# Loading x tile 2 through GpSimd's queue, and v of tile 0 ahead of tile 2's transposes, in a fused attention and gated feed-forward kernel

## The chip, the cores and the metric

The kernel runs on one core of one Trainium2 chip. The metric is the device time of one execution in microseconds. In the text PE is the matrix engine, ACT is ScalarE, DVE is VectorE, POOL is GpSimd and SP is SyncE, as the profile names them.

## The reference

The reference takes x of shape 1 x 2048 x 512 in bf16 and normalises it over its last axis. It then adds three things: x itself, a linear attention with 32 heads, and a gated feed-forward block.

```python
def _A_ref(x, wqkv, w_phi, wo):          # H = 32 heads of 16
    q, k, v = ...                        # x @ wqkv, split into heads
    pq, pk = q @ w_phi, k @ w_phi        # per head
    phi_q = concat(softmax(pq), softmax(-pq)); phi_k = the same of pk
    kv = einsum("bhsf,bhsd->bhfd", phi_k, v)
    num = phi_q @ kv; den = phi_q . sum_s(phi_k) + 1e-6
    return (num / den) @ wo

def _B_ref(x, w_gate, w_up, w_down):     # F = 1792
    return ((x @ w_gate) * (x @ w_up)) @ w_down

xn = _layernorm(A_x)
return A_x + _A_ref(xn, A_wqkv, A_w_phi, A_wo) + _B_ref(xn, B_w_gate, B_w_up, B_w_down)
```

## The kernel before

The 2048 tokens are cut into 16 tiles of 128 tokens, and the tiles are loaded into one buffer `xall`. Everything that PE multiplies needs the normalised tokens transposed (`xnT`), with the 512 features on the partitions in four blocks of 128. Four tiles form a group of 512 tokens for the feed-forward part.

The work is written in the order in which each engine runs it: inside the manual schedule the engines execute their instructions in program order, and semaphores make them wait for one another. SP is one of these engines and issues nearly all loads.

The start handles tiles 0 to 3 in a special way, because nothing else can run until they are there:

- `dma_x` (L69) loads x tiles. SP's queue issues tile 0, then tile 2, then the two halves of `wv` (L75), then the first columns of `wg` and `wu` (L72), `wphi` and the other weights. ACT's queue issues tiles 1 and 3.
- POOL builds the identity matrix `ident` for the transposes and the block pattern `BO`. PE runs warm-up matmuls on constants (`warm_up`, L308).
- The sum of each tile goes to `tots`. DVE makes the sums of tiles 0 and 3 (L373). ACT makes those of tiles 1 and 2 as a by-product of a pass whose output is thrown away (`junk`, L377).
- `sub_sum` (L337, DVE) writes 512 x minus the sum into `xn`. The scale of 512 and the standard deviation are divided out later.
- `lt(n, lo, hi, copy)` transposes blocks lo to hi of tile n on PE into a PSUM bank `tp` (L205) and copies them to `xnT` (L206) on the engine that `copy` names, ACT if none is named.
- `first_v(n, js)` runs matmuls of tile n with the blocks js of `wv` (L236). The results of tiles 0 and 1 lie in the banks that later hold the kv sums, so they carry the name `kv` in the profile; those of tiles 2 and 3 are called `pv`.
- `stats_of` (L153, L342), `scales_of` (L345, L347) and `more_scales_of` (L350, L351) make the true scale `rs` on DVE and POOL, and `first_v_out` (L361, L363) copies v with that scale.
- `make_bd` (L212, POOL) and `fold` (L225, L232) fold `w_phi` into the key weights `W1k`.

After that the feed-forward units `ffn` (one unit is four `g` matmuls, L274, four `u` matmuls, L278, a copy and a product) alternate with the projections of keys, values and queries, and then with attention and the output `fin` (L290, L293).

PSUM banks come from a ring of six (`bank`), and each new name takes the next one. The part of the start whose order matters here is:

```python
sum_of(0)
for n in (1, 2):
    nc.scalar.activation(out=junk[:], in_=xall[:, n, :], func=AF.Identity, accum_out=tots[n][:])
...
sub_sum(1, tots[1])
lt(0, 0, 2)
lt(0, 2, DC, nc.vector.tensor_copy)
lt(1)
warm_up(1)
sub_sum(2, tots[2])
sum_of(3)
sub_sum(3, tots[3])
lt(2)
for n in range(3):
    first_v(n, (0, 1))
lt(3)
```

Of the kernel before, what the change touches and what calls it, by code (L numbers as in the profile page):

```python
# [8 lines left out]
BF16 = mybir.dt.bfloat16  # L9
F32 = mybir.dt.float32  # L10
AF = mybir.ActivationFunctionType
# [10 lines left out]
def kernel(  # L22
# [12 lines left out]
    nc = tc.nc  # L35
    P = 128
    S, D = A_x.shape[-2], A_x.shape[-1]
# [4 lines left out]
    DC = D // P  # L42
# [10 lines left out]
    consts = ctx.enter_context(tc.tile_pool(name="consts", bufs=1))  # L53
# [4 lines left out]
    wv = wpool.tile([P, DC, D], BF16)  # L58
# [9 lines left out]
    def dma_x(lo, hi, eng=nc.sync):  # L68
        eng.dma_start(out=xall[:, lo:hi, :], in_=x_view[:, lo:hi, :])  # L69
# [1 line left out]
    def dma_cols(eng, w, src, lo, hi, at=0):  # L71
        eng.dma_start(out=w[:, :, lo - at:hi - at], in_=src[:, lo:hi].rearrange("(c p) f -> p c f", p=P))  # L72

    def dma_wv(lo, hi):
        nc.sync.dma_start(out=wv[:, lo:hi, :],  # L75
                          in_=A_wqkv[lo * P:hi * P, 2 * D:3 * D].rearrange("(c p) f -> p c f", p=P))

    def dma_gu(lo, hi):
        dma_cols(nc.sync, wg, B_w_gate, lo, hi)
        dma_cols(nc.sync, wu, B_w_up, lo, hi)  # L80

    dma_x(0, 1)
    dma_x(2, 3)
    dma_wv(0, 2)
    dma_wv(2, DC)
    dma_gu(0, 2 * P)
    nc.sync.dma_start(out=wphi[:], in_=A_w_phi.rearrange("(c h) d f -> (h d) c f", c=DC))
    dma_gu(2 * P, 5 * P)
# [5 lines left out]
    nc.sync.dma_start(out=wd[:], in_=B_w_down.rearrange("(c p) d -> p c d", p=P))  # L94
    nc.sync.dma_start(out=wo[:], in_=A_wo.rearrange("(c p) n -> p c n", p=P))

    ET = mybir.EngineType
    ctx.enter_context(tc.manual_schedule(engines={ET.PE, ET.DVE, ET.Activation, ET.Pool, ET.SP}))
    ones = nc.const_aps.tensor(1.0, [P, P], BF16)
    first = consts.tile([P, 1], BF16)  # L100
    nc.scalar.activation(out=first[:], in_=ones[:, 0:1], func=AF.Exp, scale=1.0)
    dma_x(1, 2, nc.scalar)
    dma_x(3, 4, nc.scalar)
    ident = consts.tile([P, P], BF16)
    make_identity(nc, ident[:])
    mhalf = consts.tile([P, GT], F32)
# [38 lines left out]
    def bank(name, dt=F32, n=TT):  # L145
        return ps_s.tile([P, n], dt, name=name, tag="s")
# [55 lines left out]
    def lt(n, lo=0, hi=DC, copy=nc.scalar.copy):  # L202
        tp = bank("tp", BF16).rearrange("p (c t) -> p c t", c=DC)
        for c in range(lo, hi):
            nc.tensor.transpose(out=tp[:, c, :], in_=xns[n][:, c * P:(c + 1) * P], identity=ident[:])  # L205
        copy(out=xnT[:, lo:hi, n * P:(n + 1) * P], in_=tp[:, lo:hi, :])  # L206
# [27 lines left out]
    def proj(ps, n, w, js=range(DC)):  # L234
        for j in js:
            nc.tensor.matmul(ps, lhsT=xnT[:, j, n * P:(n + 1) * P], rhs=w[:, j, :],  # L236
                             start=(j == 0), stop=(j == DC - 1))
# [68 lines left out]
    def warm_up(k, reps=DC):  # L306
        for _ in range(k):
            nc.tensor.matmul(warm[:, 0:reps * P], lhsT=ones,  # L308
                             rhs=nc.const_aps.tensor(1.0, [P, reps * P], BF16), start=True, stop=True)

    warm_up(7)
    warm_up(3, 1)

    with tc.tile_pool(name="ps_k", bufs=1, space=PSUM) as ps_k:
        kvbank = [ps_k.tile([P, TT], F32, name=f"kv{b}") for b in range(2)]
# [20 lines left out]
        def sub_sum(n, tot, lo=0, hi=D):  # L336
            nc.vector.tensor_scalar(out=xns[n][:, lo:hi], in0=xall[:, n, lo:hi], scalar1=float(D), scalar2=tot[:],  # L337
                                    op0=ALU.mult, op1=ALU.subtract)
# [14 lines left out]
        def first_v(n, js):  # L353
            if n not in vps:
                vps[n] = kvbank[n][:] if n < 2 else bank("pv")
            proj(vps[n], n, wv, js)
# [15 lines left out]
        def sum_of(n):  # L372
            nc.vector.tensor_reduce(out=tots[n][:], in_=xall[:, n, :], axis=AX.X, op=ALU.add)  # L373
# [4 lines left out]
        sub_sum(0, tots[0], 0, D // 2)  # L378
        sub_sum(0, tots[0], D // 2, D)
        sub_sum(1, tots[1])  # L380
        lt(0, 0, 2)
        lt(0, 2, DC, nc.vector.tensor_copy)
        lt(1)
        warm_up(1)
        sub_sum(2, tots[2])
        sum_of(3)
        sub_sum(3, tots[3])
        lt(2)
        for n in range(3):
            first_v(n, (0, 1))  # L390
        lt(3)
        first_v(0, (2, 3))
# [130 lines left out]
```

## Time and profile before

| what | value |
|---|---|
| median of 3 runs | 220.69 us (220.66 to 221.0) |
| the profiled execution | 220.62 us |
| its span | 218.9 us |
| PE busy | 214.9 us, 98% of the span |
| DVE busy | 140.6 us, 64% |
| ACT busy | 89.8 us, 41% |
| POOL busy | 74.1 us, 34% |
| granted TensorE clock | 1.0 |
| HBM read and written | 8.67 MB and 2.10 MB |

The span runs from the first to the last instruction of the program that the profiler recorded; the rest of the execution's time, 1.7 us, lies around it. Busy shares are averages over the span, so an engine with a small share can still be waited for at one place. A line number such as L205 is a line of the kernel before, and it can be the line of a helper that several callers use.

### The profile page before, as it was taken

The page shows a single profiled execution, that of the slowest core. Times are in us where ns is not written, and L with a number is a line of the kernel's source. Part 1 is how long each engine was busy: PE and PEld are TensorE (multiplying, and loading weights), DVE is VectorE, ACT ScalarE, POOL GpSimd, SP SyncE. Part 2 cuts the span into 40 slices and gives each one's busy share as a digit, 9 for nine tenths or more (in the row PEclk, how much of TensorE's full clock was granted, in tenths as well). Part 3 has the DMA queues.
Part 4 walks back from the last instruction along what each step waited for, and adds up shares of the span by engine and source line. Part 5 has one row for each costly group of instructions (what it writes and reads, how often), then busy time and mean ns, then how long its engine had stood idle before and what let it go on. Part 6 is the DMA issues. An engine that isn't in the chain of part 4 may idle for free.

```text
span 218.9 us, 3494 instructions
## 1 busy us (share of the span) xinstructions
PE 214.9 (98%) x1293; PEld 103.1 (47%) x1293; DVE 140.6 (64%) x239; ACT 89.8 (41%) x160; POOL 74.1 (34%) x71
## 2 busy tenths in 40 slices
PE   7999999999999999999999999999999999999994
PEld 3444445454444444444544444444444444454443
DVE  4868867886598758576599773296655655454321
ACT  6645686569575875565435212141231322100000
POOL 2540843363358554636045333033123033000000
PEclk9999999999999999999999999999999999999999
DMA  6999996003202540202028455114441431612301
GB/s 200 273 301 374 372 235 111 15 0 51 48 0 49 51 91 5 48 3 48 1 41 103 77 114 114 39 24 96 96 75 24 95 72 27 97 48 72 75 24 48
DMA packets 48529, 19.91 MB, mean 91 GB/s; under 512 B 37504, under 2 KB 48512, under 8 KB 48512
## 3 DMA queue, kind: packets, MB, share of 16 engines
q1 hardware_dynamic: 48224, 19.42, 39.7%
q10 hardware_dynamic: 288, 0.26, 0.3%
q8 instruction: 10, 0.16, 0.3%
q14 instruction: 7, 0.06, 0.1%
HBM read 8.67 MB, written 2.10 MB: 49 GB/s over the span
## 4 chain that ended last, share of the span: by engine, by line
PE 96%; DMA 1%; ACT 1%; DVE 0%; issue 0%
PE g L274 22%; PE fin L290 22%; PE u L278 22%; PE fin L293 6%; PE k L236 6%; PE q L236 6%; PE pv L236 6%; PE kv L330 2%; PE ab L462 2%; DMA xall<-in_A_x_dram 1%; PE kv L236 1%; ACT junk L377 1%; PE pq L225 1%; PE tp L205 0%; DVE xn L337 0%; DVE o_sb L300 0%
## 5 line engine op out<-in xcount | busy, mean ns | idle before, releaser
L274 PE MATMUL g<-xnT,wg 128*128 128x512 bf16 x224 | 57.5, 379 | 0.0
L278 PE MATMUL u<-xnT,wu 128*128 128x512 bf16 x224 | 57.5, 379 | 0.0
L282 DVE TENSOR_TENSOR hT<-u,g_sb 128x512 bf16<-128x512 f32 x56 | 37.0, 667 | 24.3 <-PE u L278 16.2
L253 POOL TENSOR_TENSOR phiq<-e,rsum 128x1024 bf16<-128x1024 f32 x16 | 30.9, 1933 | 63.5 <-DVE rsum L251 56.0
L281 ACT CAST g_sb<-g 128x512 bf16<-128x512 f32 x56 | 32.9, 587 | 47.1 <-PE g L274 46.9
L249 DVE TENSOR_REDUCE sums<-e 128x64 f32<-128x1024 f32 x32 | 38.9, 1216 | 20.1 <-ACT e L246 20.1
L290 PE MATMUL fin<-wd,hT 128*128 128x512 bf16 (+2 forms) x238 | 51.1, 366 | 0.0
L253 POOL TENSOR_TENSOR phik<-e,rsum 128x1024 bf16<-128x1024 f32 x16 | 30.9, 1932 | 40.0 <-DVE rsum L251 37.9
L278 PEld LDWEIGHTS <-wu 128*128 128x128 bf16 x224 | 21.9, 98 | 26.4
L290 PEld LDWEIGHTS <-hT 128*128 128x128 bf16 x238 | 22.5, 98 | 24.7
L274 PEld LDWEIGHTS <-wg 128*128 128x128 bf16 x224 | 21.1, 98 | 24.0
L236 PEld LDWEIGHTS <-xnT 128*128 128x128 bf16 x192 | 17.5, 98 | 18.3 <-ACT xnT L206 0.3
L300 DVE TENSOR_TENSOR o_sb<-fin,xall 128x512 bf16<-128x512 f32 (+2 forms) x13 | 8.5, 651 | 20.5 <-PE fin L293 20.5
L251 DVE RECIPROCAL rsum<-sums 128x64 f32<-128x64 f32 x32 | 17.7, 553 | 3.1
L293 PE MATMUL fin<-wo,oT 128*128 128x512 bf16 (+2 forms) x68 | 16.6, 366 | 0.0
L236 PE MATMUL k<-W1k,xnT 128*128 128x512 bf16 x64 | 16.4, 379 | 0.0
L236 PE MATMUL q<-W1q,xnT 128*128 128x512 bf16 x64 | 16.4, 378 | 0.0
L245 ACT ACTIVATE e<-q 128x512 f32<-128x512 f32 x12 | 7.2, 597 | 22.2 <-PE q L236 22.2
L236 PE MATMUL pv<-wv,xnT 128*128 128x512 bf16 x56 | 14.4, 379 | 0.0
L475 DVE TENSOR_TENSOR otok<-ab,rden 128x512 bf16<-128x512 f32 x16 | 11.1, 692 | 0.6
L322 ACT CAST vt<-pv 128x512 bf16<-128x512 f32 x12 | 7.0, 587 | 10.0 <-PE pv L236 10.0
L153 DVE BATCH_NORM_STATS2 stats<-xall 128x6 f32<-128x512 bf16 x16 | 10.6, 665 | 0.0
(62 smaller groups left out, 130.6 us busy)
## 6 DMA issues: line engine op xcount, KB each, us to landing
out_dram<-o_sb SPq DMA_DIRECT2D x15, 128.0 KB, 2.0
wd<-in_B_w_down_dram SPq DMA_DIRECT2D x1, 1792.0 KB, 15.5
xall<-in_A_x_dram SPq DMA_DIRECT2D x1, 1024.0 KB, 11.4
wg<-in_B_w_gate_dram SPq DMA_DIRECT2D x1, 640.0 KB, 8.5
wu<-in_B_w_up_dram SPq DMA_DIRECT2D x1, 640.0 KB, 9.7
wv<-in_A_wqkv_dram SPq DMA_DIRECT2D x2, 256.0 KB, 4.1
xall<-in_A_x_dram SPq DMA_DIRECT2D x1, 512.0 KB, 4.3
wg<-in_B_w_gate_dram SPq DMA_DIRECT2D x1, 512.0 KB, 5.2
```

Of the source, the lines that this page charges most:

```text
L153: nc.vector.bn_stats(out=stats[:], in_=xall[:, n, :])
L236: nc.tensor.matmul(ps, lhsT=xnT[:, j, n * P:(n + 1) * P], rhs=w[:, j, :], start=(j == 0), stop=(j == DC - 1))
L249: nc.vector.tensor_reduce(out=sums[:], in_=ev, axis=AX.X, op=ALU.add)
L251: nc.vector.reciprocal(out=rsum[:].rearrange("p a b -> p (a b)"), in_=sums[:])
L253: nc.gpsimd.tensor_tensor(out=phi[:].rearrange("p g (x f) -> p (g x) f", f=DH), in0=ev, in1=rsum[:].to_broadcast((P, 2 * H, DH)), op=ALU.mult)
L274: nc.tensor.matmul(gps, lhsT=wg[:, c, f * P:(f + 1) * P], rhs=xnT[:, c, T * TT:(T + 1) * TT], start=(c == 0), stop=(c == DC - 1))
L278: nc.tensor.matmul(ups, lhsT=wu[:, c, f * P:(f + 1) * P], rhs=xnT[:, c, T * TT:(T + 1) * TT], start=(c == 0), stop=(c == DC - 1))
L281: nc.scalar.copy(out=g_sb[:], in_=gps)
L282: nc.vector.tensor_tensor(out=hTs[T][:, f, :], in0=ups, in1=g_sb[:], op=ALU.mult)
L290: nc.tensor.matmul(ps, lhsT=hTs[T][:, f, t4 * P:(t4 + 1) * P], rhs=wd[:, f, lo:lo + w], start=(f == 0), stop=False)
L293: nc.tensor.matmul(ps, lhsT=oTs[n][:, c, :], rhs=wo[:, c, lo:lo + w], start=False, stop=(c == DC - 1))
L475: nc.vector.tensor_tensor(out=o_tok[:].rearrange("p (b h d) -> p b h d", b=2, d=DH), in0=abv[:, :, :, 0:DH], in1=rden[:].to_broadcast((P, ...
```

## The change

Tile 2 of x is no longer issued by SP but by GpSimd's queue, as that engine's first instruction of the kernel's own. SP's queue therefore issues the two halves of `wv` right behind tile 0, and the manual schedule begins ahead of the other loads. The two halves of tile 0's transposes swap the engines that copy them. The first two matmuls of v of tile 0 go ahead of the transposes of tile 2. These are done in two halves, the first copied by ACT and the second by DVE, and DVE's copy lies between its sum and its subtraction of tile 3. Two more short warm-up matmuls are run at the start.

```diff
-    def dma_wv(lo, hi):
-        nc.sync.dma_start(out=wv[:, lo:hi, :],
-                          in_=A_wqkv[lo * P:hi * P, 2 * D:3 * D].rearrange("(c p) f -> p c f", p=P))
+    def dma_wv(lo, hi, eng):
+        eng.dma_start(out=wv[:, lo:hi, :],
+                      in_=A_wqkv[lo * P:hi * P, 2 * D:3 * D].rearrange("(c p) f -> p c f", p=P))
...
     dma_x(0, 1)
-    dma_x(2, 3)
-    dma_wv(0, 2)
-    dma_wv(2, DC)
+    dma_wv(0, 2, nc.sync)
+    dma_wv(2, DC, nc.sync)
+
+    ET = mybir.EngineType
+    ctx.enter_context(tc.manual_schedule(engines={ET.PE, ET.DVE, ET.Activation, ET.Pool, ET.SP}))
+    ones = nc.const_aps.tensor(1.0, [P, P], BF16)
+    first = consts.tile([P, 1], BF16)
+    nc.scalar.activation(out=first[:], in_=ones[:, 0:1], func=AF.Exp, scale=1.0)
+    dma_x(1, 2, nc.scalar)
+    dma_x(3, 4, nc.scalar)
+    dma_x(2, 3, nc.gpsimd)
     dma_gu(0, 2 * P)
...
     warm_up(7)
-    warm_up(3, 1)
+    warm_up(5, 1)
...
-        lt(0, 0, 2)
-        lt(0, 2, DC, nc.vector.tensor_copy)
+        lt(0, 0, 2, nc.vector.tensor_copy)
+        lt(0, 2, DC)
         lt(1)
         warm_up(1)
+        first_v(0, (0, 1))
         sub_sum(2, tots[2])
+        lt(2, 0, 2)
         sum_of(3)
+        lt(2, 2, DC, nc.vector.tensor_copy)
         sub_sum(3, tots[3])
-        lt(2)
-        for n in range(3):
+        for n in (1, 2):
             first_v(n, (0, 1))
         lt(3)
         first_v(0, (2, 3))
```

More of the change, by code (lines that the diff above doesn't have):

```diff
@@ L95 @@
     nc.sync.dma_start(out=wo[:], in_=A_wo.rearrange("(c p) n -> p c n", p=P))
[L97 to L103, printed above, removed]
     ident = consts.tile([P, P], BF16)
```

## The prediction

> **What bounds the kernel now.** I read the page first, then the chain of waits in order of time up to 9.6 us, then the timelines of PE, ACT and DVE from 3 to 7 us, then the DMA answers for the first loads.
>
> The page's slices and its chain by engine:
>
> ```profile
> PE   7999999999999999999999999999999999999994
> ...
> PE 96%; DMA 1%; ACT 1%; DVE 0%; issue 0%
> ```
>
> PE is full in every slice but the first and the last, and the chain that ended last is 96% PE. So only the piece ahead of the first feed-forward matmul can still move. The chain through that piece (start, length, what):
>
> ```profile
> 0.85 2.74 DMA xall<-in_A_x_dram
> ...
> 3.61 0.46 ACT junk L377
> 4.07 0.08 issue
> 4.15 0.19 ACT junk L377
> 4.34 0.02 issue
> 4.37 0.73 ACT junk L377 x2
> 5.10 0.05 issue
> 5.15 0.36 DVE xn L337
> 5.51 0.05 issue
> 5.55 0.40 PE tp L205 x4
> 5.95 0.86 PE kv L236 x4
> ```
>
> x tile 1 lands at 0.85 + 2.74 = 3.59; ScalarE sums tile 1, then tile 2 (`junk`); VectorE subtracts the mean of tile 2; PE transposes tile 2 at 5.55, and from there PE never waits. Tile 2 itself was there earlier: issued on SP at 1.24, 2.8 us to landing, so 4.04, while ScalarE got to it at 4.37. PE's timeline around the last hole:
>
> ```profile
> 5.12 0.38 PE L308 MATMUL warm<-const-bfloat16-1.0 128*128 128x512 bf16 x1
> 5.55 0.40 PE L205 MATMUL tp<-ident,xn 128*128 128x128 bf16 x4
> ...
> 9.46 1.03 PE L274 MATMUL g<-xnT,wg 128*128 128x512 bf16 x4
> ```
>
> Matmuls of 512 columns follow each other every 0.216 us (four in 0.86), transposes every 0.056. After the warm-up matmul PE is free at 5.12 + 0.216 = 5.33 and idles 0.22 until 5.55. From 5.55 to 9.46 it runs 16 matmuls and 8 transposes: 3.45 + 0.45 = 3.90. From 9.46 on PE runs 206 us without a wait for data, so the change is worth what it moves the start of the first `g` from 9.46, one for one, unless it opens a hole behind.
>
> **The change, part by part.** *v of tile 0 ahead of tile 2's transposes.* Two matmuls (0.43) go into the hole: 5.33 to 5.76. Tile 2's `xn`, ready at 5.55, then waits for PE instead of the other way round, and 14 matmuls and 8 transposes remain: 3.02 + 0.45 = 3.47. The first `g` starts at 5.76 + 3.47 = 9.23, a gain of 0.22 to 0.23. That needs three things at 5.3: the last warm-up, columns 0 and 1 of `xnT` for tile 0, and the first half of `wv`.
>
> *Copies of tile 0 swapped.* The half that v of tile 0 needs first goes to DVE. Before, DVE copied at 4.94 (0.29) and ACT at 5.00 (0.35), ACT being held by its sum of tile 2. Now DVE can copy right behind the subtraction of tile 1, which starts at 4.48 and takes 0.35: about 4.8 to 5.1, ahead of 5.3. DVE's next step, the subtraction of tile 2, waits for ScalarE until 5.15 anyway. Cost nothing; if that copy came behind the ACT sum as before, it would be ready at 5.35, and 0.05 would be lost.
>
> *wv earlier on SP.* Its first half is issued at 1.24 instead of 1.71 (3.9 us to landing, so 5.61 before). The DMA engines decide, not the issue:
>
> ```profile
> 1.80:2.20 0.40, 0.40 (x3) 0.14 (x1) 0.00 (x0) 0.39 (x2) 0.33 (x2) 1.00 0.38 128
> 2.20:2.60 0.40, 0.40 (x3) 0.12 (x2) 0.00 (x0) 0.09 (x1) 0.20 (x1) 1.00 0.79 274
> 2.60:3.00 0.40, 0.40 (x3) 0.13 (x2) 0.00 (x0) 0.00 (x0) 0.00 (x0) 1.00 1.12 333
> ```
>
> The last two columns are DMA share and GB/s: unfilled until 2.6, full after. Before, four x tiles and the first half of `wv` (768 KB) had landed by 5.61, `wv` last. Now `wv` follows x0 at once and shares with x1, x3 and x2 instead of following x2. It cannot be later than 5.61 if the engines stay as full, and if three queues share evenly its data is through some 0.4 to 0.6 us before that: I take a landing at 5.1, bounds 4.8 and 5.6. Up to 5.3 it costs nothing; at 5.6 v of tile 0 starts at 5.65 instead of 5.33, and the sum is +0.1 instead of -0.22.
>
> *x2 through GpSimd's queue.* No row shows a load issued there. GpSimd's first own work starts at 0.78, so the issue is near that. Lower bound: 2.5 us to landing, x0's row, gives 3.3. Upper bound: the longest small load of the start, `wphi` (16 KB, 4.8), gives 5.6. I take 3.5, the longest x row (3.1) plus 0.4 for 128 KB at 333 GB/s among three sharers, because the x rows have the same bytes at the same moment: 4.3. ScalarE reaches tile 2 at 4.37; from landing to tile 2's transposes the rows give 5.55 - 4.37 = 1.18. So no cost up to a landing of 5.76 - 1.18 = 4.57 (from 4.37 to there PE is busy with v of tile 0), none compared with before up to 9.46 - 3.47 - 1.18 = 4.80, and one for one from there: 0.82 slower at the bound of 5.6. Behind the issue on GpSimd are `ident` (done at 1.35, first used at 4.42: 3 us of room) and `BO` (done at 2.40, needed by `bd` at 12.27).
>
> The rows show VectorE idle from 1.62, the end of its five memsets, to 3.36. The Trainium skill, page "SBUF — State Buffer", section "SBUF: two separate sides", says that a DMA from GpSimd's queue waits while VectorE is in a two-port mode, since GpSimd cannot write the descriptors then. No run here shows it yet; it stands as a rival below.
>
> *x1 and x0 among three queues.* By 2.6 the SP queue had moved 114 packets and ScalarE's 53; 80 packets then left in 0.2 us. x1 has some 75 left: at a half share 0.44 us, at a third 0.56, so x1 lands about 0.1 later (bounds 0 and 0.2). The subtraction of tile 1 and the transposes and warm-up behind it slip by 0.05, and tile 2's `xn` is ready at 5.65, still hidden by v of tile 0. ScalarE's copy of tile 1 ends near 6.0, where v of tile 1 wants it: 0.02 more. Together I charge 0.07.
>
> *Tile 2's copy on two engines.* The ACT half costs 0.35 instead of 0.58; v of tile 2 wants it at 6.45 and gets it at 6.4 to 6.5. The DVE half (0.29) stands between the sum and the subtraction of tile 3, so `xn` of tile 3 comes at 6.8 instead of 6.48; PE wants it at 6.9. Hidden; without that cover 0.29 at most. The statistics behind it on DVE shift by 0.3, and with them GpSimd's scales, the v copies on DVE (last end 11.77) and `bd` (end 13.35, needed at 14.74). DVE waits 0.82 for PE before its product at 13.19, which swallows the shift.
>
> *The rest.* Two more warm-ups of 128 columns cost 0.11 in a hole from 4.14 to 4.42: nothing. SP's later issues wait, as far as I read the gap from 4.84 to 5.62 that ends as `wv` lands, for an earlier load's signal; the second weights may so be issued up to 0.8 later, against use at 12.9 and landings near 10 to 11: nothing.
>
> Sum: -0.22 + 0.07 = -0.15. The profiled execution took 220.62 (span 218.9 and 1.7 around it), 0.07 under the median of 220.69; so 220.47 by it, 220.54 by the median. I say 220.5.
>
> **The rivals.**
>
> *Tile 2 arrives late (slower).* The place is ScalarE's sum of tile 2, the point 4.80, the price one for one, up to +0.82. For it: the whole chain from 4.37 to 5.55 hangs on this tile, the path is unmeasured, and now every ScalarE copy of tiles 0 and 1 queues behind that sum. If GpSimd's descriptors had to wait for the last VectorE memset at 1.62, x2 would land 0.84 later, at 5.14: +0.34. (That is the rule of the page "SBUF — State Buffer" of the Trainium skill.) With a slower queue on top, 5.3 to 5.6: +0.5 to +0.8, 221.2 to 221.5. Against it: VectorE is idle when the transfer should run. Chance 0.24, two thirds of it beyond 5.24, where the loss passes 0.2%.
>
> *v of tile 0 waits for wv.* Put ahead of the transposes, it now blocks them. With the engines full, `wv` could still be last, at 5.6: +0.1, 220.8. Against it: it is issued 0.46 earlier and shares evenly. Chance 0.09.
>
> *More than the hole.* If the unfilled DMA time before 2.6 is used by the third queue and x0 and x1 both land 0.25 earlier, the whole front moves: -0.47, 220.2. Against it: x0's packets start at 1.8 whatever stands in the other queues. Chance 0.07.
>
> **How the numbers follow.** The forecast, a gain between 0 and 0.25, has 0.60. 0.2% is 0.44 us, about what a measurement of this kernel can tell from no change. Faster by more: 0.07, the last rival. Slower by more: 0.16, from late tile 2. Within: 0.60 + 0.09 + 0.08 = 0.77. The range goes from 220.3 (best gain, and the spread of the runs) to 221.1 (tile 2 at 5.24); the likeliest case alone would be 220.4 to 220.7.
>
> **What would show it.** Right: PE's transposes of tile 2 start behind two `kv` matmuls near 5.8 and the first `g` near 9.3; PE without a hole after 5.4; x2 landing before 4.6 and `wv` before 5.3. Wrong: `junk` of tile 2 starting after 4.6 with DMA as its releaser (tile 2 late); an idle PE ahead of `kv` ended by DMA (`wv` late); the hole between transposes of tile 0 and of tile 1 growing (x0, x1 late); a hole ahead of `tp` of tile 3 ended by DVE (the copy split). The forecast also falls if PE shows a hole after 9.5, or if the time around the span changes from 1.7.

## The result and the profile after

The changed kernel takes 221.44 us (median of 17 runs, 221.09 to 222.28) against 221.0 for the kernel before (17 runs, 220.41 to 221.21). The ratio over all these runs is 1.0026, 95% interval 1.0017 to 1.0035, which is 0.57 us of 221; the medians lie 0.44 apart. The three runs that the prediction started from (220.69) lay low in the spread of the kernel before.

The profiled execution took 221.36, span 219.7. From here a line of the kernel before has a number higher by one or so (L377 is now L378). The chain of waits of the changed kernel up to the first `g`:

```profile
1.29 4.07 DMA xall<-in_A_x_dram
...
5.46 0.73 ACT junk L378 x2
6.19 0.03 issue
6.21 0.37 DVE xn L338
6.58 0.05 issue
6.63 0.40 PE tp L206 x4
7.02 0.56 PE kv L237 x2
```

The chain no longer starts with tile 1 on ScalarE's queue but with tile 2 on GpSimd's: issued at 1.29, landed 4.07 later, at 5.37. ScalarE's sum of it starts at 5.46 (4.37 before), and its transposes at 6.63 (5.55 before). PE's timeline:

```profile
4.98 0.38 PE L309 MATMUL warm<-const-bfloat16-1.0 128*128 128x512 bf16 x1
5.20 0.59 PE L237 MATMUL kv<-wv,xnT 128*128 128x512 bf16 x2
6.63 0.40 PE L206 MATMUL tp<-ident,xn 128*128 128x128 bf16 x4 [0.83 <-DVE xn L338]
6.98 0.60 PE L237 MATMUL kv<-wv,xnT 128*128 128x512 bf16 x2
...
10.23 0.59 PE L275 MATMUL g<-xnT,wg 128*128 128x512 bf16 x2
```

v of tile 0 is where it was meant to be, at 5.20 with no wait behind the warm-up. Its second matmul starts at 5.41 and takes 0.22, so PE stands still from 5.63 to 6.63 (the bracket's 0.83 counts from the 0.59 of the row before), the bracket names DVE's `xn`, and the first `g` starts at 10.23 instead of 9.46: 0.77 later. ScalarE's timeline names the cause:

```profile
5.46 0.63 ACT L378 ACTIVATE junk<-xall 128x512 bf16<-128x512 bf16 x1 [1.26 <-DMA xall<-in_A_x_dram]
```

It was idle for 1.26 until the load. Behind the first `g` nothing changed. The profiled time less the start of the first `g` is 220.62 - 9.46 = 211.16 before and 221.36 - 10.23 = 211.13 after, and it lies between 211.1 and 211.2 in every execution profiled below. So time and first `g` can be read for one another throughout.

### The profile page after: what moved, and what is told of

Its sections match the earlier page's. It is cut to its first block, busy times and chain, and to the rows that moved or that the text cites. A ratio compares the mean times of both kernels' runs of the same rounds, so it can differ in the third digit from the quotient of the medians.

```text
span 219.7 us, 3476 instructions
## 1 busy us (share of the span) xinstructions
PE 213.9 (97%) x1271; PEld 103.4 (47%) x1295; DVE 140.7 (64%) x240; ACT 89.5 (41%) x160; POOL 74.9 (34%) x72
## 4 chain that ended last, share of the span: by engine, by line
PE 95%; DMA 2%; issue 1%; ACT 0%; DVE 0%; POOLq 0%; ACTq 0%
PE g L275 22%; PE u L279 22%; PE fin L291 22%; PE fin L294 6%; PE q L237 6%; PE k L237 6%; PE pv L237 6%; PE ab L465 2%; PE kv L331 2%; DMA xall<-in_A_x_dram 2%; PE kv L237 1%; PE pq L226 1%; ACT junk L378 0%; PE tp L206 0%; DVE xn L338 0%
## 5 line engine op out<-in xcount | busy, mean ns | idle before, releaser
L275 PE MATMUL g<-xnT,wg 128*128 128x512 bf16 x215 | 56.5, 379 | 0.5
L279 PE MATMUL u<-xnT,wu 128*128 128x512 bf16 x220 | 56.8, 379 | 0.2
L237 PE MATMUL k<-W1k,xnT 128*128 128x512 bf16 x60 | 15.7, 379 | 0.1
```

Of the source, the lines that this page charges most:

```text
L275: nc.tensor.matmul(gps, lhsT=wg[:, c, f * P:(f + 1) * P], rhs=xnT[:, c, T * TT:(T + 1) * TT], start=(c == 0), stop=(c == DC - 1))
L279: nc.tensor.matmul(ups, lhsT=wu[:, c, f * P:(f + 1) * P], rhs=xnT[:, c, T * TT:(T + 1) * TT], start=(c == 0), stop=(c == DC - 1))
```

## The experiments

### What makes tile 2 late

Theory A: the path through GpSimd has a fixed delay. B: VectorE locks GpSimd out. C: GpSimd's own next instructions hold the transfer back. D: the DMA engines are full of the other queues' packets. The six runs of this part edit the changed kernel and were each executed once, under the profiler, so they are read by issues, first packets and landings and not by their times.

**BO built late**, so little stands behind the load on GpSimd.

```diff
-    nc.gpsimd.memset(BO[:], 1.0)
-    _block_rows(nc.gpsimd, BO[:], 8, DH, E1)
...
+        nc.gpsimd.memset(BO[:], 1.0)
+        _block_rows(nc.gpsimd, BO[:], 8, DH, E1)
         for n in range(GT):
             more_scales_of(n)
```

> The changed kernel with the block pattern BO built late: its memset and two selections go from the start of GpSimd's own work to just ahead of the scales' multiples, so behind tile 2's load GpSimd has only the identity to build (done at 2.65 in the changed kernel, where BO lasted until 3.70). In the changed kernel the load is issued at 1.30, its instruction ends at 2.06, its first packet moves at 3.99, it lands at 5.37. Theory A (the path has a delay of its own): first packet again 2.6 to 2.8 after the issue, landing 5.2 to 5.5. Theory C (GpSimd's next instructions hold the transfer back until they are done): first packet at about 2.9, landing at about 4.3, first g about 1 earlier than 10.24. Theories B (VectorE) and D (full DMA engines): as A.

Measured: GpSimd was done with the identity at 2.65, the first packet moved at 3.84, the load landed at 5.63, first `g` at 10.50. The first packet came as late as with `BO` in front, so C is not what holds it.

**VectorE's memsets late.**

```diff
-    nc.vector.memset(mhalf[:], -0.5)
...
-        nc.vector.memset(vt[:, :, :, DH:E1], 1.0)
...
         sub_sum(3, tots[3])
+        nc.vector.memset(mhalf[:], -0.5)
+        for vt in vts:
+            nc.vector.memset(vt[:, :, :, DH:E1], 1.0)
```

> The changed kernel with VectorE's six memsets (0.86 to 1.63) moved behind its subtraction of tile 3, so VectorE does nothing until x tile 0 lands. Theory B (VectorE's memsets keep GpSimd from writing descriptors or from starting): issue near 0.8 instead of 1.30 and first packet 0.5 to 0.8 earlier than 3.99. Theory A: issue at 1.3 and first packet at 4.0 as in the changed kernel. Theories C and D: as A.

Measured: issue again at 1.29, first packet at 3.94, landing at 5.14, first `g` at 10.00. The memsets neither delay the issue nor the first packet.

**VectorE kept busy.**

```diff
+    dsc = consts.tile([P, 2, D], BF16)
+    nc.vector.memset(dsc[:, 0, :], 0.0)
+    for _ in range(10):
+        nc.vector.tensor_copy(out=dsc[:, 1, :], in_=dsc[:, 0, :])
```

> The changed kernel with a memset of 128x512 and ten copies of 128x512 bf16 from SBUF to SBUF on VectorE ahead of its first sum, on a scratch tile that nothing else reads, so VectorE is busy from 1.0 to beyond 3. Theory B (the rule that VectorE's two-port work locks out GpSimd's descriptor writing): the load's instruction, 0.77 long in the changed kernel, gets longer by the copies that it meets, or its first packet moves from 3.99 to behind the last copy; landing later than 5.37 by 0.5 or more. Theory A: instruction still about 0.77, first packet still about 2.7 after the issue. VectorE's own sum of tile 0 may start later, which delays the first g in either case and is not the point.

Measured: first packet at 4.04, landing at 5.30. GpSimd's timeline in this run, with VectorE copying from 1.91 on:

```profile
1.29 0.77 POOL L69 DMA_DIRECT2D xall<-in_A_x_dram  x1 [0.79 <-POOLq L515]
2.05 0.29 POOL masks.py:197 MEMSET ident<- 128x128 bf16 x1
2.42 0.29 POOL masks.py:199 TENSOR_SCALAR_AFFINE_SELECT ident<-ident 128x128 bf16<-128x128 bf16 x1
2.66 0.35 POOL L117 MEMSET BO<- 128x136 bf16 x1
```

The load's instruction keeps its 0.77, while the memsets take 0.29 and 0.35 where the changed kernel has 0.22 and 0.21. So VectorE's copies do slow GpSimd (every execution without them has 0.20 to 0.23 for these two), but this load is no later: B falls here. The rule of the Trainium skill that the prediction names ("SBUF — State Buffer", section "SBUF: two separate sides") would fit the longer memsets and is not seen in the load. Of VectorE's scratch work only the memset and the first 0.14 of a copy overlapped the load's instruction, so a longer overlap was not tried.

**wv and all behind it wait.** x tile 3 goes to SP as well, so that only tiles 0, 1 and 2 are in flight at first.

```diff
     dma_x(0, 1)
-    dma_wv(0, 2, nc.sync)
-    dma_wv(2, DC, nc.sync)
...
+    dma_x(2, 3, nc.gpsimd)
+    nc.vector.tensor_copy(out=wv[:, 0, 0:1], in_=xall[:, 0, 0:1])
     dma_x(1, 2, nc.scalar)
-    dma_x(3, 4, nc.scalar)
-    dma_x(2, 3, nc.gpsimd)
+    dma_wv(0, 2, nc.sync)
+    dma_wv(2, DC, nc.sync)
+    dma_x(3, 4, nc.sync)
```

> The changed kernel in which SP's loads behind x tile 0 (wv and all the rest, and x tile 3, moved to SP) wait until VectorE has written one element of wv after tile 0's landing at 3.2, so from 1.8 to 3.6 only tiles 0, 1 and 2 are in flight and the DMA engines have room. Theory D (the transfer waits behind the other queues' packets): first packet at 2.6 to 3.2 instead of 3.99, landing at 3.8 to 4.2. Theory A: first packet still 2.6 to 2.8 after the issue, near 4.0; landing perhaps 0.2 to 0.4 earlier than 5.37, as its packets meet fewer others. The first g comes late because wv comes late, in any case.

Measured: the issue again at 1.29 with 0.77, but the first packet at 2.88 and the landing at 4.34. The DMA answer up to 3.9 us, by queue (packets, MB, share), first for the changed kernel:

```profile
q1 hardware_dynamic: 357, 0.35, 32.9%
q10 hardware_dynamic: 238, 0.23, 16.6%
```

and for this run:

```profile
q0 software_dynamic: 46, 0.13, 11.5%
q1 hardware_dynamic: 144, 0.13, 10.2%
q10 hardware_dynamic: 144, 0.13, 9.7%
```

q1 is SP's queue, q10 ScalarE's, q0 GpSimd's. In the changed kernel q0 has no line: by 3.9 the other two had moved 595 packets and tile 2 none. With little else in flight 46 of its 48 had gone. So D holds for about 1.03 of the landing (5.37 - 4.34). What is left is the path itself: issue at 1.29, and 0.83 from the end of the instruction (2.05) to the first packet. The page "DMA: Bandwidth & Descriptors" of the Trainium skill, section "Queues, rings and completion order", has each DMA engine take turns between its queues packet by packet. The 595 to 0 do not look like taking turns.

This run also says what the three before it could not. In those the load waited for the other queues until 3.8 to 4.0 in any case, so a delay by GpSimd or VectorE that ends sooner would not show. Here the first packet moved at 2.88 while GpSimd went on with the identity and `BO` until 3.69, so C falls. Whether VectorE's copies would delay the load on engines as quiet as these was not tried.

**wphi second.** A 16 KB load is put ahead of `wv` on SP, so that `wv` is issued after tile 2 and not before.

```diff
     dma_x(0, 1)
+    nc.sync.dma_start(out=wphi[:], ...)
     dma_wv(0, 2, nc.sync)
...
-    nc.sync.dma_start(out=wphi[:], ...)
```

> The changed kernel with wphi (16 KB) moved up to SP's second load, so the first half of wv is issued at 1.7 instead of 1.25, behind GpSimd's load of tile 2 (1.29) and ScalarE's of tile 3 (1.26). Theory E (the DMA engines serve transfers roughly in the order in which they were issued, whatever the queue): tile 2 no longer has wv's 256 KB in front of it; first packet at 2.9 to 3.3 instead of 3.99, landing at 4.4 to 4.7, tile 3 near 4.3, wv at 5.3 to 5.7. Theory D' (the queues share evenly, only the total in flight counts): tile 2 within 0.3 of 5.37. Theory A (GpSimd's path alone): 5.1 to 5.6.

Measured: first packet at 3.31, and up to 3.9:

```profile
q0 software_dynamic: 33, 0.10, 8.3%
```

So the order of issue does decide when tile 2 starts (theory E): in the six executions in which GpSimd's load was issued at 1.29, with `wv` and one x tile ahead of it, its first packet moved at 3.81 to 4.04. That `wphi` comes in many small packets could have helped it, but the run below with tile 2 on SP and tile 3 on GpSimd's queue also has `wv` behind GpSimd's load, without that, and there the first packet moved at 2.93. So even sharing falls. The landing did not follow: it came at 5.49, and in the five of the six that load tile 2 this way it came at 5.14 to 5.63. Of its 16 parts 14 had landed by 4.77 (5.11 in the changed kernel), the last two at 5.45 and 5.49. A load counts when its slowest part is there, and why those two were late stays open. First `g` at 10.36; `wv` landed at 6.17 and held v of tile 0 until 6.21.

**Identity first, then the load.**

```diff
-    dma_x(2, 3, nc.gpsimd)
...
     make_identity(nc, ident[:])
+    dma_x(2, 3, nc.gpsimd)
```

> The changed kernel with GpSimd building the identity first (0.78 to 1.35 in the kernel before) and issuing tile 2's load behind it. If the load's start at 1.29 is the moment from which this queue is ready, whatever came before, the identity costs it little: issue at 1.3 to 1.5, landing at 5.3 to 5.6. If every load on this queue needs half a microsecond ahead of its issue (0.78 to 1.29 in the changed kernel): issue at 1.8 to 1.9; then by theory E (order of issue) wv's second half, issued at 1.72, is also ahead of it and it lands at 6.0 to 6.5; by even sharing at 5.8 to 5.9.

Measured: issue at 1.47, right behind the identity (done at 1.36), landing at 5.82, first `g` at 10.69. So the half microsecond after 0.78 is not added behind GpSimd's earlier work; it fits a queue that is ready near 1.3. Whether a second load would pay it again no run here shows.

### The two halves of the change apart

**The queue alone**: the kernel before with tile 2 on GpSimd's queue.

```diff
-    dma_x(2, 3)
...
     dma_x(3, 4, nc.scalar)
+    dma_x(2, 3, nc.gpsimd)
```

> The kernel before with x tile 2 loaded by GpSimd's queue, issued as that engine's first instruction of its own, and nothing else changed. Theory A: tile 2 lands near 5.4, its transposes start near 6.6 instead of 5.55, and with v of tile 0 not yet done PE has 3.90 of work left: first g at 10.5, 1.05 later than before; ratio 1.004 to 1.005, worse than the whole change by the 0.43 less a hole of some 0.15. Rival (the loss comes from the new order): first g below 9.7, ratio within 1.001.

Measured: 221.92 against 220.94, ratio 1.0033 (1.002 to 1.0047); tile 2 at 5.24. The median run has its first `g` near 221.92 - 211.14 = 10.8, as forecast within 0.3; the ratio fell short of the 1.004 to 1.005 expected. The profiled execution took 223.21, more than the median:

```profile
5.34 0.63 PE L308 MATMUL warm<-const-bfloat16-1.0 128*128 128x512 bf16 x1
6.49 0.61 PE L205 MATMUL tp<-ident,xn 128*128 128x128 bf16 x4 [0.51 <-DVE xn L337]
6.89 1.91 PE L236 MATMUL kv<-wv,xnT 128*128 128x512 bf16 x4
```

Four matmuls in 1.91 instead of 1.03: the matrix engine ran at half speed until 9.9.

**All but the queue**: the changed kernel with tile 2 as SP's second load.

```diff
     dma_x(0, 1)
+    dma_x(2, 3)
-    dma_x(2, 3, nc.gpsimd)
```

> The changed kernel with x tile 2 back on SP's queue, right behind tile 0 and ahead of wv, so all of the change but the queue. Theory A (all of the loss is the late tile 2): tile 2 lands near 4.0; first g at 9.2 to 9.6 depending on wv, which lands near 5.6 as before and then holds v of tile 0 back; time 0.1 to 0.2 us either side of the kernel before (ratio 0.999 to 1.001). Rival (the new order of the start costs something by itself): first g at 9.8 or later, ratio 1.002 or more.

Measured: ratio 1.0005 (0.9983 to 1.0028), an interval that holds both no change and the 1.0026 of the whole change; the runs went from 220.84 to 221.73, with a median of 221.40 against 220.94. So this run by itself does not show that the new order is free. In the profiled execution (221.58) tile 2 landed at 4.03, but PE waited for `wv`, which landed at 6.23:

```profile
6.27 0.79 PE L237 MATMUL kv<-wv,xnT 128*128 128x512 bf16 x2 [0.29 <-DMA wv<-in_A_wqkv_dram]
```

That is the second rival of the prediction, v of tile 0 held by `wv` in front of the transposes.

### Looking for an order in which both loads are there

**Tiles 1, 2, 3 on ScalarE's queue.**

```diff
-    dma_x(3, 4, nc.scalar)
-    dma_x(2, 3, nc.gpsimd)
+    dma_x(2, 3, nc.scalar)
+    dma_x(3, 4, nc.scalar)
```

> The changed kernel with tiles 1, 2 and 3 all on ScalarE's queue in that order, nothing on GpSimd's. Theory A: tile 2 lands at 4.2 to 4.5, before the point of 4.57; wv before 5.2; v of tile 0 starts near 5.3, first g at 9.2 to 9.35; ratio to the kernel before 0.9990 to 0.9995, the gain that was forecast for the whole change. Rival (wv or tile 1 is slowed by three queues' worth of x): first g at 9.46 or later, ratio 1.000 or more.

Measured: ratio 1.003 (1.0015 to 1.0044). In the profiled execution (220.87, first `g` 9.75) tile 2, issued just behind `wv`, landed at 4.75 (4.2 to 4.5 expected), `wv` at 4.80, and tile 3 at 6.13. The median run took 0.9 more than this execution; why was not profiled.

**The same with wphi second on SP**, so that tile 2 is issued ahead of `wv`.

> Tiles 1, 2 and 3 on ScalarE's queue as in the run with all three there, and wphi (16 KB) as SP's second load, so tile 2 (issued at 1.26) is ahead of wv (1.7) and tile 3 (1.74) about level with it. Theory E (order of issue): tile 2 lands at 4.0 to 4.4 instead of 4.80, wv's first half at 5.0 to 5.5; first g at 9.2 to 9.6 where the matrix clock is up by 5.5. Theory D' (even sharing): tile 2 within 0.2 of 4.80, first g near 9.75. Time: first g plus 211.14, as in all profiled executions so far; ratio to the kernel before 0.998 to 1.000 by E, 1.001 to 1.003 by D'.

Measured: tile 2 at 4.09, as E has it, but `wv` at 6.21 and v of tile 0 at 6.25; ratio 1.0021 (1.001 to 1.0032). The landing was forecast, the time was missed.

**Tile 3 on GpSimd's queue, tile 2 second on ScalarE's.**

> The changed kernel with tiles 2 and 3 swapped between the queues: tile 2 is ScalarE's second load, tile 3 goes through GpSimd's queue. Theory A: tile 3 lands near 5.4, just as VectorE reaches its sum at about 5.4, so the late landing costs 0 to 0.3; tile 2 lands at 4.3 to 4.8; first g at 9.2 to 9.5; ratio 0.999 to 1.000. Rival (any load on GpSimd's queue slows the whole start, by its packets or by GpSimd's delayed work): first g beyond 9.7.

Measured: ratio 1.000 (0.999 to 1.001). Tile 2 at 4.81, `wv` at 4.98, tile 3 at 5.25:

```profile
5.49 0.59 PE L237 MATMUL kv<-wv,xnT 128*128 128x512 bf16 x2
6.07 0.40 PE L206 MATMUL tp<-ident,xn 128*128 128x128 bf16 x4
```

The loads, the queues and the new order are those of the changed kernel, and undoing only the choice of which tile goes the slow way removes the loss. With the queue alone at 1.0033 this shows that the late tile 2 is the cause of the loss. It gives no gain, as the transposes of tile 2 are at 6.07, not 5.76.

**Tile 2 second on SP, tile 3 on GpSimd's queue.**

> The changed kernel with tile 2 back as SP's second load, wv behind it, tile 1 alone on ScalarE's queue, and tile 3, which VectorE needs only at 5.4, on GpSimd's. Theory E: order x0, x1, x2, then tile 3 and wv; tile 2 at 3.9 to 4.1, wv's first half at 5.0 to 5.5 (128 KB less ahead of it than with tile 3 on ScalarE's queue, unless GpSimd's load comes first), tile 3 at 5.0 to 5.4; first g at 9.25 to 9.6, ratio 0.998 to 1.000. Rival (wv holds v of tile 0 back as with tile 2 on SP and tile 3 on ScalarE, where it landed at 6.23): wv at 5.6 or later, first g at 9.7 or later, ratio 1.000 to 1.002.

Measured: tile 2 at 3.73, but `wv` at 6.97 and tile 3 at 6.33; first `g` at 11.00, ratio 1.0035 (1.0017 to 1.0053). The rival's side, and worse than it said.

**Tile 3 behind wv on SP**, nothing on GpSimd's queue, with the new order and then with the old one.

```diff
     dma_x(0, 1)
+    dma_x(2, 3)
     dma_wv(0, 2, nc.sync)
+    dma_x(3, 4)
     dma_wv(2, DC, nc.sync)
...
-    dma_x(3, 4, nc.scalar)
-    dma_x(2, 3, nc.gpsimd)
```

> The changed kernel with SP loading tile 0, tile 2, the first half of wv, tile 3, then the second half of wv; ScalarE's queue loads tile 1 alone, GpSimd's nothing. Theory E (service in order of issue): tile 2 lands at 3.7 to 4.1, the first half of wv at 4.8 to 5.4 (128 KB less ahead of it), tile 3 at 5.0 to 5.6. If the order is worth what was forecast, v of tile 0 starts at 5.3 to 5.4, first g at 9.25 to 9.5, ratio to the kernel before 0.998 to 0.9995, and 0.2 less than g2. Rival (the slowest DMA engine decides, and wv still lands near 6): first g at 9.7 or later, ratio 1.000 to 1.002, no better than g2.

> The kernel before with the same loads as g1 and nothing else changed: v of tile 0 stays behind tile 2's transposes. Tile 2's transposes start at 5.5 to 5.6 whatever wv does, wv is there when v needs it at 5.8, first g at 9.4 to 9.6; tile 3 at 5.0 to 5.6 is late for VectorE's sum at 5.41 by at most 0.2, which the old order hides behind three v steps. Ratio 0.9990 to 1.0005. Rival (wv near 6): v of tile 0 starts at 6.1 to 6.3 and the first g comes at 9.8 or later.

Measured: 0.9994 (0.9982 to 1.0005) with the new order and 0.9992 (0.9984 to 1.0001) with the old. The loads may be worth a little; the order adds nothing that shows. PE in the run with the new order, tile 2 landed at 3.85 and `wv` at 5.59:

```profile
5.30 0.63 PE L309 MATMUL warm<-const-bfloat16-1.0 128*128 128x512 bf16 x1
5.73 0.98 PE L237 MATMUL kv<-wv,xnT 128*128 128x512 bf16 x2
6.55 0.39 PE L206 MATMUL tp<-ident,xn 128*128 128x128 bf16 x4
```

and with the old order, `wv` at 5.93:

```profile
5.10 0.38 PE L308 MATMUL warm<-const-bfloat16-1.0 128*128 128x512 bf16 x1
5.54 0.40 PE L205 MATMUL tp<-ident,xn 128*128 128x128 bf16 x4
5.97 1.02 PE L236 MATMUL kv<-wv,xnT 128*128 128x512 bf16 x4
```

In the first PE was still at half speed (0.63 for the warm-up, 0.98 for two matmuls), in the second at full speed (0.38). The warm-up at half speed occupies PE until 5.30 + 0.43 = 5.73: there is no hole to fill. At full speed the hole is there, from 5.32 to 5.54, but `wv` is not.

### How typical the profiled execution was

> The kernel before, unchanged, profiled once more. Theory F (the moment at which the matrix engine goes to full speed differs from execution to execution, about evenly between 3.9 and 7.3, and the first profile was at the early end): full speed at 4.5 to 7, the hole ahead of tile 2's transposes 0 to 0.1 instead of 0.22, first g at 9.6 to 10.2, time again first g plus 211.14, so 220.7 to 221.3. Rival (the first profile was typical): full speed near 3.9, hole 0.2, first g at 9.46 give or take 0.1.

> The kernel before, unchanged, a further profile. The same two theories as for the one ahead of it: by F full speed anywhere from 4.5 to 7 and most likely not where the last one had it, first g at 9.6 to 10.2; by the rival full speed near 3.9 and first g near 9.46.

Measured: 220.42 with the first `g` at 9.29, and 220.90 with 9.76. PE went to full speed at 4.2 and at 5.1. In the execution that the prediction used it did so at 3.8, the earliest of all executions profiled here, as theory F has it, and only one of the 17 runs of the kernel before was below its 220.62. But the execution with 4.2 is faster still: its hole was as wide (5.16 to 5.38), and tile 1 had landed at 3.41 instead of 3.59. So the speed alone does not set the start. In the slower one tile 2, still on SP, landed at 4.60 instead of 4.03. One kernel's start moves by 0.5 from one execution to the next.

**No warm-up matmuls at all.**

```diff
-    warm_up(7)
-    warm_up(3, 1)
...
-        warm_up(1)
```

> The kernel before without any warm-up matmul (the ten at the start and the one before tile 2's transposes), so PE's first work is the transposes at 4.4. Theory F: half speed until a full stretch of 3.4 us of work has passed, so until 7.5 to 11.5; 24 matmuls or more at 0.427 instead of 0.216, first g at 11 to 13 and some g at half speed behind it; ratio 1.008 to 1.02. Rival (the speed of the start hardly matters, because loads decide): first g below 10.3, ratio under 1.004.

Measured: ratio 1.0072 (1.0051 to 1.0093), just under the range expected; half speed until 9.5, first `g` at 11.53. So 1 to 2 us of the start hang on when full speed comes.

## Why the prediction was wrong

It forecast -0.15 and the change cost 0.57; in the two profiled executions the first `g` moved by +0.77 instead. The step that failed is *x2 through GpSimd's queue*, by its landing: 4.3 was taken, 5.37 measured, inside the bounds of 3.3 to 5.6. The issue was put near 0.78 and was at 1.29 (0.51). From issue to landing 3.5 was taken, the longest x row (3.1) plus 0.4 for an even share among three; it was 4.07 (0.57). With little else in flight the same load took 3.06 (1.29 to 4.34), so the 3.1 was right and the 0.4 was mis-sized: sharing cost 1.0. The even share is what the runs refute: tile 2 sent nothing until 3.99, behind `wv` and tile 3, which were issued 0.04 and 0.03 before it.

From there the working held, but for one slip: the 1.18 runs from the start of ScalarE's sum and not from the landing, and 0.09 lay between the two. The sum of tile 2 started 0.89 past 4.57, the point up to which it would have cost nothing (5.46). Tile 2's transposes followed 1.17 later (1.18 forecast), and 3.47 of work led to the first `g` with 0.12 on top, where v of tile 1 waited for ScalarE's copy of tile 1, queued behind that sum. 5.46 + 1.17 + 3.47 + 0.12 = 10.22, and the first `g` was at 10.23. The first rival named this place, the point of 4.80 and, for a landing at 5.3 to 5.6, +0.5 to +0.8; it had a chance of 0.24 and was the case. Its place and price held. The reason that it worked out, descriptors that wait for VectorE's memsets, did not: with the memsets moved the issue stayed at 1.29 and the first packet at 3.94. That the landing fell where it had put it is in part luck.

- *v of tile 0 into the hole.* It ran at 5.20, 0.13 earlier than forecast, with `wv` at 5.01 (5.1 forecast). The gain of 0.22 that it should bring needs tile 2 by 4.57 and `wv` by 5.3 at once, and no profiled order had both. With tile 2 ahead, `wv` landed at 5.5 to 7.0; with `wv` ahead, at 4.8 to 5.1, and tile 2 at 4.75 or later. The term was mis-sized even without GpSimd: the old order fills the time in which `wv` is still on its way.
- *x0 and x1 among three queues.* 0.07 was charged; they landed at 3.20 and 3.45, against 3.33 and 3.59 in the first profile of the kernel before and 3.16 to 3.26 and 3.41 to 3.43 in its two repeats. So no cost and no gain shows.
- *Copies, extra warm-ups, tile 2's copy in two halves, `ident` and `BO`, later weights.* Nothing of them shows: tile 0's first copy was done at 4.98, and PE has no hole behind the first `g` that the kernel before lacks.
- *The range.* It ended at a landing of 5.24, and the base of 220.69 was 0.3 under the median of 17 runs. The base alone would have been covered (221.0 is under 221.1), the loss alone would not (220.69 + 0.57 = 221.26).

## What to carry to other kernels

Here the DMA engines were full (busy share 0.92 from 2 to 4 us in the changed kernel, 1.02 from 4 to 6), and moving a load to another queue gave it no bandwidth, only another place in line: in such a place list what is issued ahead of it, count those bytes, and expect its first packet behind them and the slowest of its parts later still. A queue that the trace has never shown should carry the load with the most slack (tile 3 here, ratio 1.000 with `wv` still ahead of it), not the one that heads the chain (tile 2, 1.0026). Filling a hole pays only if what fills it is ready, so the fill's own loads belong in the sum with the same weight as the load it waits for.

## What the runs showed of the hardware

- A load on GpSimd's queue was issued at 1.29 in each run that put it first, though GpSimd's memset started at 0.78 where there was none; with the identity ahead (done at 1.36) it was at 1.47.
- The moment from which the matrix engine runs at full speed differs between executions. It shows in the spacing of matmuls, 0.427 before it against 0.216 after it at 512 columns, and the trace's record of the granted clock begins there: at 3.83 in the first profile of the kernel before, at 4.44 in the changed kernel, at 12.15 with VectorE kept busy. The views count the time ahead of that record as 1.00, so a granted clock of 1.00 at the start tells nothing. In 16 of the 19 executions profiled the record lasts 215.04, and in the three with the latest moments (9.48, 9.92 and 12.15) 211.63, which is 3.41 less. A moment that can only fall on steps of 3.41 would fit that; it was not tested.
- Of a load's 16 parts the last one or two can come 0.4 to 1.0 us after the others (tile 3 in the second repeat of the kernel before: 15 parts by 4.23, the last at 5.26; `wv` in the run with tile 2 on SP: 5.43 and 6.23). In the run with tile 2 on SP the two loads behind it have one late part as well (6.15 and 6.98, 7.05 and 7.90), so it looks like one DMA engine that stays behind and not like a matter of one load. Which engine, and why, stays open.
